# One core, all steps in a newly planned order: an attention block and a gated linear unit on TensorE

## The chip, the core and the metric

The kernel runs on one NeuronCore of one Trainium2 chip. A core has five engines that run their own instruction streams: TensorE (matmuls; PE in the profile, with its weight loads as PEld), VectorE (DVE), ScalarE (ACT), GpSimd (POOL) and SyncE (SP, here only a queue of DMA issues). They meet through semaphores. The metric is the device time of one execution in microseconds (us). The kernel before takes 303.13 us (median of three runs, 302.70 to 303.86).

## The reference

Inputs: q, k, v of shape (8 batches, 8 heads, 576 tokens, 64), a gain g_norm of 64, two 512x512 weights, and five rows of convolution weights of 512. The weights come in as 64-bit floats, and the kernel narrows them to 32 bits by integer arithmetic on the chip.

```python
kv  = einsum('bhsd,bhse->bhde', k, v)
out = einsum('bhsd,bhde->bhse', q, kv)
rms = sqrt(mean(out * out, axis=-1, keepdims=True) + 1e-06)
x   = (out / rms * g_norm)  # then (B, H, S, D) -> (B, S, H*D) = (8, 576, 512)

gate_pre[:, s] = sum over k of conv_w[k] * x[:, s - 4 + k]   # causal, zeros before s = 0
gate = 1.0 / (1.0 + exp(-gate_pre))
val  = x @ w_val
y    = (gate * val) @ w_out
```

## The kernel before, in words

Everything is in fp32. The work is cut into 1242 *steps*, each a small Python function that issues a few instructions. One string, PLAN, lists the steps in order, and a loop at the end of the kernel (`for step in PLAN.split(";")`) runs them as they stand there. No scheduler moves anything afterwards: each engine and each DMA queue executes its own instructions in the order of PLAN. The numbers behind an `@` say which buffers a step takes: PSUM banks (8 of them), tiles for normalised x (3), for output rows (`ot`, 4), for gates (4), and so on. If a buffer is still in use the step waits for its last reader.

The steps of one batch b, in the order of their data:

- **Loads.** `load_half k b i` and `load_half v b i` bring half the heads each. `load_q_rows` (batches 0 and 1) and `load_q` (the others, in four DMAs) bring q. `stage_weight` brings a quarter of a weight. Nearly all are issued on SP's queue, where the output stores are too.
- **k·v on quarters.** `kv_product b i` (line 475) has 36 small matmuls that use a 64x64 quarter of the array each; `kv_copy` (ACT) takes the result out. 
- **q·kv on quarters.** `turn_q` transposes q on DVE (in batch 1 `turn_q_rows` does it on PE, with half-width 128x64 matmuls, line 520). `raw_pair b c` (32 matmuls) and `raw_tail b` (8) are 64x64 as well (line 550). Batch 0 goes over `raw_half` (line 562).
- **Norm.** `square` (ACT), `sums` (DVE), `powers` (POOL, line 616), `normalise` (ACT, 16 small scalings to a `raw_pair`, line 635).
- **x transposed.** Batches 0 and 1 and all tails: `turn_x` on PE (line 647) and `keep_x` (ACT). Else `turn_blocks` (DVE) and `move_blocks` (8 DMAs to a batch's quarter set, on SP and POOL).
- **Gate.** `halo` (POOL), `gate_start` (ACT), four `gate_tap` (DVE, line 685), `gate_end` (ACT), `gated` (DVE).
- **Value product.** `val_product` (line 697) in batches 0 and 1; later `val_fast` in seven parts with `x_sums` on DVE ahead (a scheme with fewer multiplications) and `val_keep` behind, on ACT and DVE (line 746).
- **Output product.** To a pair of batches i: `token_sums` (DVE), then for each group p `fast_product i p 0..6` (line 837, full array) and `fast_keep i p 0..6` (ACT and DVE); `out_product i 8` (line 784, half-width) for the tail rows; `store`.

A `fast_product` of a group adds into the same bank as an earlier one: part 2 must come after `fast_keep` 0 has read the bank, part 4 after `fast_keep` 2, part 6 after `fast_keep` 4. Parts 1, 3 and 5 share another bank.

```python
        bank, tokens, weights_ = (        # fast_product, parts 0 to 6
            ("a", chunk(0, EVEN), wout[:, EVEN, LOW]), ("c", total(0), wsum[:, 0]),
            ("a", total(1), wsum[:, 1]), ("b", chunk(0, ODD), wout[:, ODD, LOW]),
            ("a", total(2), wsum[:, 2]), ("c", total(3), wout[:, ODD, HIGH]),
            ("a", chunk(1, ODD), wsum[:, 3]))[n]
```

(`b` and `c` are halves of one bank.) Three kinds of PE steps can be told apart by what they occupy: the **full array** (`turn_x`, `val_product`, `val_fast`, `fast_product`, most `raw_half`), **64x64 quarters** (`kv_product`, `raw_pair`, `raw_tail`), and **other part-width shapes** (`turn_q_rows` of batch 1, `out_product`, the tail of `raw_half`, `start_warm`, `turn_cw`). In this text an *excursion* is a stretch of PE's order in which it leaves full-array matmuls and comes back to them.

Of the kernel before, what the change touches and what calls it, by code (L numbers as in the profile page):

```python
# [31 lines left out]
narrow_weight wval 1 6 @ 1; load_half v 1 0; raw_half 0 4 0 @ 2; narrow_weight wval 0 3; sums 0 3 @ 0 0;
load_half k 1 1; raw_half 0 4 1; square 0 2 @ 1; narrow_weight wval 0 4; raw_half 0 0 0; powers 0 3;
narrow_weight wval 1 1; load_half v 1 1; raw_half 0 1 1; narrow_weight wval 0 7; square 0 4 @ 2;
square 0 0 @ 0; sums 0 2; narrow_weight wval 1 2; sums 0 4; load_half k 2 0 @ 0; normalise 0 3 @ 0;
narrow_weight wval 1 3; powers 0 2; sums 0 0; turn_q_rows 1 3 @ 0; square 0 1 @ 1; narrow_weight wval 1 4;
turn_x 0 3 @ 7; narrow_weight wval 3 0 @ 1; sums 0 1; turn_q_rows 1 0 @ 3; keep_x 0 3; load_half v 2 0 @ 0;
narrow_weight wval 3 1; normalise 0 2 @ 1; powers 0 1; turn_q_rows 1 1 @ 5; narrow_weight wval 1 7;
narrow_weight wval 3 2; load_half v 2 1 @ 0; turn_x 0 2 @ 7; normalise 0 4 @ 2; narrow_weight wval 3 3;
narrow_weight wval 2 5 @ 2; turn_x 0 4 @ 4; narrow_weight wval 2 0 @ 0; turn_q_rows 1 2 @ 2; keep_x 0 4;  # L40
narrow_weight wval 3 5 @ 0; keep_x 0 2; narrow_weight wval 3 6 @ 3; narrow_weight wval 2 1;
val_product 0 1 1 @ 4; narrow_weight wval 3 4; halo 0; narrow_weight wval 2 2; normalise 0 0 @ 0;
narrow_weight wval 2 3; normalise 0 1 @ 1; narrow_weight wval 3 7; sort_q 1 0 @ 1; turn_x 0 1 @ 7; sort_q 1 3;
narrow_weight wout 0 0 @ 1; turn_x 0 0 @ 6; narrow_weight wval 2 4; kv_product 1 0 @ 3 1; keep_x 0 0;
narrow_weight wout 0 5 @ 1; keep_x 0 1; narrow_weight wval 2 6 @ 0; gate_start 0 0 @ 0;
narrow_weight wout 0 6 @ 3; val_product 0 1 0 @ 0; narrow_weight wval 2 7; gate_start 0 2 @ 1;
narrow_weight wout 1 0 @ 0; gate_start 0 1 @ 2; gate_tap 0 0 3; narrow_weight wout 1 1; val_product 0 3 1 @ 6;
gate_tap 0 2 3; narrow_weight wout 0 1; gate_tap 0 1 3; narrow_weight wout 1 2; val_sums 2; gate_start 0 3 @ 3;
turn_q_rows 1 4 @ 7; gate_tap 0 2 2; sort_q 1 2; kv_product 1 1; load_q 2 1; gate_tap 0 3 3; gate_tap 0 1 2;
val_product 0 3 0 @ 2; kv_copy 1 1; kv_copy 1 0; sort_q 1 1; gate_tap 0 0 2; stage_weight wout 3 @ 0;  # L50
narrow_weight wout 0 2; load_q 2 2; gate_tap 0 1 1; narrow_weight wout 0 3; narrow_weight wout 1 5 @ 2;
raw_pair 1 3 @ 1 3; val_sums 0; sort_q 1 4; keep_val 0 1 0; narrow_weight wout 1 3; gate_tap 0 3 2; load_q 2 0;
raw_tail 1 @ 7 5; val_product 0 0 1 @ 0; keep_val 0 1 1; gate_tap 0 1 0; keep_val 0 3 1; square 1 4 @ 2;
gate_tap 0 3 1; square 1 3 @ 0; square 1 2 @ 1; sums 1 4 @ 1 1; raw_pair 1 1 @ 4 6; gate_tap 0 3 0;
keep_val 0 3 0; powers 1 4; gate_end 0 1; sums 1 2; val_product 0 2 0 @ 2; square 1 0 @ 2; sums 1 3;
keep_val 0 0 1; gated 0 1; normalise 1 4 @ 2; powers 1 3; val_sums 1; gate_end 0 3; turn_x 1 4 @ 0;
narrow_weight wout 3 5 @ 1; kv_product 2 0 @ 5 7; sums 1 0; keep_x 1 4; keep_val 0 2 0; powers 1 2;
square 1 1 @ 1; narrow_weight wout 1 4; val_product 0 2 1 @ 0; normalise 1 3 @ 1; narrow_weight wout 0 4;
sums 1 1; stage_weight wout 2 @ 1; narrow_weight wout 1 6 @ 0; load_half v 3 0 @ 0; powers 1 1;
normalise 1 2 @ 0; load_half k 3 0 @ 0; turn_x 1 3 @ 2; turn_q 2 1 @ 0; kv_product 2 1; gate_tap 0 0 1;  # L60
keep_x 1 3; powers 1 0; turn_x 1 2 @ 1; gate_tap 0 0 0; normalise 1 1 @ 2; val_product 0 0 0 @ 3;
narrow_weight wout 3 6 @ 2; turn_q 2 0; keep_x 1 2; halo 1; narrow_weight wout 0 7; normalise 1 0 @ 1;
load_q 2 3; turn_x 1 1 @ 2; narrow_weight wout 3 0 @ 1; val_product 1 3 1 @ 1; narrow_weight wout 1 7;
narrow_weight wout 2 0 @ 0; narrow_weight wout 3 1; gate_tap 0 2 1; load_half v 3 1 @ 0;
narrow_weight wout 2 1; load_half k 3 1 @ 0; narrow_weight wout 2 5 @ 1; val_product 1 0 1 @ 4; gate_tap 0 2 0;
keep_val 1 3 1; narrow_weight wout 3 2; val_sums 3; narrow_weight wout 3 3; gated 0 3; kv_copy 2 1;
val_product 1 2 1 @ 6; narrow_weight wout 2 2; turn_q 2 2; gate_end 0 2; turn_q 2 3; kv_copy 2 0;
keep_val 0 2 1; narrow_weight wout 3 4; gate_end 0 0; load_q 3 2; turn_x 1 0 @ 1; gated 0 2;
raw_pair 2 3 @ 7 5; keep_val 0 0 0; keep_val 1 2 1; gated 0 0; narrow_weight wout 2 3; raw_pair 2 1 @ 3 0;
square 2 3 @ 0; load_q 3 0; token_sums 0 0 0 @ 2; keep_val 1 0 1; val_product 1 1 1 @ 6; token_sums 0 0 1;  # L70
keep_x 1 0; keep_x 1 1; sums 2 3 @ 0 0; square 2 0 @ 2; load_q 3 1; narrow_weight wout 2 4; powers 2 3;
square 2 1 @ 1; weight_sums 0; val_product 1 2 0 @ 4; keep_val 1 1 1; sums 2 0; square 2 2 @ 0;
narrow_weight wout 3 7; gate_start 1 2 @ 2; powers 2 0; sums 2 1; kv_product 3 0 @ 2 1; keep_val 1 2 0;
sums 2 2; gate_start 1 0 @ 3; gate_tap 1 2 3; val_product 1 1 0 @ 6; normalise 2 3 @ 0; powers 2 2;
load_half k 4 0 @ 0; gate_tap 1 0 3; narrow_weight wout 2 6 @ 3; load_half v 4 0 @ 0; token_sums 0 0 2 @ 0;
powers 2 1; normalise 2 2 @ 2; fast_product 0 1 0 @ 4; narrow_weight wout 2 7; kv_product 3 1; weight_sums 1;
keep_val 1 1 0; turn_q 3 2 @ 1; raw_tail 2 @ 7 5; val_product 1 0 0 @ 6; weight_sums 2; square 2 4 @ 2;
kv_copy 3 0; turn_blocks 2 3; kv_copy 3 1; normalise 2 0 @ 1; turn_blocks 2 2; turn_q 3 0;
fast_product 0 1 1 @ 2; normalise 2 1 @ 0; turn_blocks 2 0; load_q 3 3; fast_product 0 1 3; gate_tap 1 0 2;
val_product 1 3 0 @ 1; fast_keep 0 1 0 @ 0; turn_q 3 1; gate_start 1 1 @ 1; turn_blocks 2 1; sums 2 4;  # L80
move_blocks 2 1; token_sums 0 0 3; fast_product 0 0 0 @ 0; keep_val 1 3 0; gate_tap 1 1 3; move_blocks 2 3;
fast_product 0 0 1 @ 3; fast_keep 0 0 0 @ 2; gate_tap 1 0 1; fast_keep 0 1 1 @ 1; gate_start 1 3 @ 0;
move_blocks 2 0; fast_product 0 0 3; gate_tap 1 0 0; keep_val 1 0 0; move_blocks 2 2; fast_product 0 1 5;
turn_q 3 3; gate_end 1 0; fast_product 0 1 2; weight_sums 3; fast_keep 0 0 1 @ 3; load_q 4 2; powers 2 4;
gate_tap 1 1 2; raw_pair 3 3 @ 1 6; fast_keep 0 1 2; gated 1 0; fast_product 0 0 2; square 3 2 @ 1;
gate_tap 1 1 1; square 3 3 @ 0; fast_keep 0 1 5; load_half v 4 1 @ 0; fast_product 0 1 4; normalise 2 4 @ 2;
sums 3 2 @ 1 1; fast_product 0 0 5; load_q 4 0; gate_tap 1 3 3; powers 3 2; turn_x 2 4 @ 2; fast_keep 0 1 4;
raw_pair 3 1 @ 7 5; keep_x 2 4; sums 3 3; fast_keep 0 0 2; x_sums 2 0 @ 0; fast_product 0 1 6; square 3 0 @ 2;
powers 3 3; store 0 2; gate_tap 1 3 2; square 3 1 @ 1; val_fast 2 1 0 @ 2; fast_keep 0 0 5; fast_keep 0 1 6;
# [824 lines left out]
```

## Time and profile before

| what | us |
|---|---|
| median of the runs | 303.13 |
| the profiled execution | 303.11 |
| its span, first to last instruction | 301.3 |
| PE busy | 290.3 |
| DVE busy | 272.0 |
| ACT busy | 194.5 |
| POOL busy | 114.1 |

Times in the views count from the start of the span. A PE row that is busy is not proof of useful work, since matmuls are pipelined and overlap: what counts is how far one start lies behind the one before. DMA moved 55.5 MB, at 359 GB/s in the first 30 us and at 184 on the mean.

### The profile page before, as it was taken

How to read it: one execution, taken by the hardware profiler on the slowest of the kernel's cores; microseconds unless marked ns; L12 is line 12 of the kernel's file. 1: busy time of each engine (PE TensorE's matmuls, PEld its weight loads, DVE VectorE, ACT ScalarE, POOL GpSimd, SP SyncE). 2: the span in 40 equal slices, each digit the busy share in tenths (PEclk: the TensorE clock that was granted, in tenths of full speed). 3: DMA queues.
4: the chain of work that ended last, by engine and by line, in shares of the span. 5: the costliest groups of instructions: out<-in, count | busy, mean ns of one | idle time of the engine just before them, and what ended most of it. 6: DMA issues, size and time to landing. Idle time of an engine off the chain costs nothing.

```text
span 301.3 us, 8755 instructions
## 1 busy us (share of the span) xinstructions
PE 290.3 (96%) x3333; PEld 227.9 (76%) x3333; DVE 272.0 (90%) x483; ACT 194.5 (65%) x606; POOL 114.1 (38%) x127
## 2 busy tenths in 40 slices
PE   6969999999999999999999999999999999999993
PEld 3658778778887768778778857788887588888572
DVE  2699999999999999999999899999999999999612
ACT  2887999998767957838864666557489244524320
POOL 3046029346578049218740296400693080000000
PEclk9998999999999999999999999999999999999999
DMA  7999686985678756966986669671650172311343
GB/s 266 373 385 413 245 244 203 297 228 184 154 191 222 243 146 143 315 180 165 268 208 221 184 140 303 173 208 30 165 115 17 34 168 70 82 43 29 94 114 105
DMA packets 32073, 55.51 MB, mean 184 GB/s; under 512 B 6166, under 2 KB 14358, under 8 KB 32032
## 3 DMA queue, kind: packets, MB, share of 16 engines
q1 hardware_dynamic: 29520, 49.76, 56.0%
q0 software_dynamic: 1632, 3.17, 4.9%
q10 hardware_dynamic: 880, 2.03, 1.8%
q8 instruction: 26, 0.43, 0.6%
q14 instruction: 15, 0.12, 0.1%
HBM read 39.21 MB, written 9.44 MB: 161 GB/s over the span
## 4 chain that ended last, share of the span: by engine, by line
PE 82%; DMA 12%; SPq 3%; ACT 1%; issue 0%; DVE 0%; ACTq 0%
PE bank L837 28%; PE bank L746 24%; PE bank L697 11%; DMA qs<-in_q_dram 7%; PE bank L550 6%; PE bank L475 5%; PE bank L784 5%; DMA out_dram<-ot 3%; DMA v<-in_v_dram 2%; PE bank L647 2%; PE bank L520 2%; SPq L869 1%; SPq L381 1%; SPq L366 1%; ACT ot L851 0%
## 5 line engine op out<-in xcount | busy, mean ns | idle before, releaser
L685 DVE SCALAR_TENSOR_TENSOR gate<-xT,cwT,gate 128x576 f32<-128x576 f32 x128 | 101.3, 807 | 0.9
L616 POOL TENSOR_TENSOR rt<-ss,mhalf 128x8 f32<-128x8 f32 (+3 forms) x38 | 70.1, 1854 | 59.6 <-DVE ss L606 59.5
L635 ACT ACTIVATE x<-bank,rt 128x64 f32<-128x64 f32 x252 | 55.8, 365 | 6.8 <-POOL rt L616 6.7
L668 POOL DMA_DIRECT2D xT<-y x48 | 26.6, 559 | 72.5 <-PE bank L837 38.4
L837 PE MATMUL bank<-wsum,w 128*128 128x256 f32 x192 | 47.0, 383 | 0.9 <-ACT ot L853 0.8
L837 PEld LDWEIGHTS bank<-wsum,w 128*128 128x128 f32 x192 | 35.6, 190 | 7.9 <-ACT ot L853 1.9
L746 PE MATMUL bank<-xs,vsum 128*128 128x288 f32 x144 | 38.5, 407 | 0.0
L697 PE MATMUL bank<-xT,wval 128*128 128x288 f32 x128 | 33.9, 413 | 0.0
L837 PE MATMUL bank<-wout,gv 128*128 128x256 f32 x128 | 32.6, 380 | 0.3 <-ACT ot L851 0.3
L746 PEld LDWEIGHTS bank<-xs,vsum 128*128 128x128 f32 x144 | 27.1, 190 | 7.3 <-DVE gv L753 0.2
L599 ACT ACTIVATE sq<-bank 128x256 f32<-128x256 f32 (+1 forms) x70 | 21.0, 374 | 12.9 <-PE bank L550 12.8
L697 PEld LDWEIGHTS bank<-xT,wval 128*128 128x128 f32 x128 | 23.4, 190 | 6.3 <-ACT xT L654 0.2
L837 PEld LDWEIGHTS bank<-wout,gv 128*128 128x128 f32 x128 | 24.2, 190 | 4.3 <-ACT ot L851 0.4
L606 DVE TENSOR_REDUCE ss<-sq 128x8 f32<-128x520 f32 (+1 forms) x40 | 24.8, 627 | 2.2 <-ACT sq L599 2.2
L746 PE MATMUL bank<-xT,wval 128*128 128x288 f32 x96 | 26.4, 408 | 0.0
L847 DVE TENSOR_TENSOR ot<-bank,ot 128x512 f32<-128x512 f32 (+1 forms) x32 | 17.1, 548 | 10.1 <-DMA out_dram<-ot 9.2
L679 ACT ACTIVATE gate<-xT,cwT 128x576 f32<-128x576 f32 x32 | 25.7, 809 | 0.5 <-DVE gv L710 0.2
L692 ACT ACTIVATE gate<-gate 128x576 f32<-128x576 f32 x32 | 22.1, 704 | 5.0 <-DVE gate L685 5.0
L710 DVE TENSOR_TENSOR gv<-gv,gate 128x576 f32<-128x576 f32 x32 | 23.5, 750 | 1.0 <-ACT gate L692 0.7
L746 PEld LDWEIGHTS bank<-xT,wval 128*128 128x128 f32 x96 | 18.0, 190 | 4.5 <-ACT x L635 0.2
L550 PEld LDWEIGHTS bank<-kv,qT 64*64 64x64 f32 x1008 | 16.3, 135 | 5.7 <-issue 3.7
L475 PEld LDWEIGHTS bank<-v,k 64*64 64x64 f32 x1008 | 16.0, 135 | 4.0 <-issue 1.6
(93 smaller groups left out, 454.0 us busy)
## 6 DMA issues: line engine op xcount, KB each, us to landing
qs<-in_q_dram SPq DMA_DIRECT2D x96, 140.0 KB, 3.8
out_dram<-ot SPq DMA_DIRECT2D x140, 64.0 KB, 1.8
k<-in_k_dram SPq DMA_DIRECT2D x14, 576.0 KB, 5.4
v<-in_v_dram SPq DMA_DIRECT2D x12, 576.0 KB, 6.3
xT<-y SPq DMA_DIRECT2D x48, 64.0 KB, 2.6
xT<-y POOLq DMA_DIRECT2D x48, 64.0 KB, 2.4
y<-in_moe_w_val_dram SPq DMA_DIRECT2D x4, 512.0 KB, 11.6
w<-in_moe_w_out_dram SPq DMA_DIRECT2D x4, 512.0 KB, 7.4
```

Of the source, the lines that this page charges most:

```text
L475: nc.tensor.matmul(st["kvps", b][s][r * D:(r + 1) * D, i], st["k", b, i][rows, r, cols], st["v", b, i][rows, r, cols], start=(j == 0), sto ...
L550: nc.tensor.matmul(st["raw", b, c][r][cols, to * D:(to + 1) * D], st["qT", b][rows, hp, first:first + D], kvs[b % 2][rows, hp, :], start=T ...
L606: nc.vector.reduce_sum(out=st["ss", b][:, FIRST[c]:FIRST[c] + n], in_=st["sq", b, c][:, 0:n], axis=AX.X)
L616: nc.gpsimd.tensor_tensor(out=st["rt", b][:, which], in0=st["ss", b][:, which], in1=mhalf[:, which], op=ALU.pow)
L635: nc.scalar.activation(out=x[:, to * D:(to + 1) * D], in_=raw[:, h * D:(h + 1) * D], func=AF.Copy, scale=root[:, to:to + 1])
L668: (nc.sync if i % 2 else nc.gpsimd).dma_start(out=xTs[b % 2][i * TB:(i + 1) * TB, :, first:first + P], in_=y[a * TB:(a + 1) * TB, i])
L679: nc.scalar.activation(out=gate[:], in_=xTs[b % 2][:, jt, HALO:SX], func=AF.Copy, scale=cwT[:, K - 1, jt:jt + 1])
L685: nc.vector.scalar_tensor_tensor(out=gate[:], in0=xTs[b % 2][:, jt, tap * TB:tap * TB + S], scalar=cwT[:, tap, jt:jt + 1], in1=gate[:], op ...
L697: nc.tensor.matmul(val[:], wval[:, kc, jt * P:(jt + 1) * P], xTs[b % 2][:, kc, HALO + n * SV:HALO + (n + 1) * SV], start=(kc == 0), stop=( ...
L710: nc.vector.tensor_tensor(out=both, in0=both, in1=st["gate", b, jt][:], op=ALU.mult)
L746: nc.tensor.matmul(st[bank, "val", b, mj][:], weights_[:, k], tokens()[:, k], start=(n in (0, 1, 3) and k == 0), stop=(k == NK // 2 - 1), ...
L837: nc.tensor.matmul(st[bank, i, p], tokens()[:, k], weights_[:, k], start=(n < 2 and k == 0), stop=(k == NK // 2 - 1), skip_group_check=True)
```

## The change

The functions stay as they are. PLAN is replaced as a whole: it has the same 1242 steps with the same arguments in another order, with other buffers behind the `@`. The first eleven steps and the last eight are as before.

What the new order does, read out of both:

- **Excursions.** PE's order before has 30: 22 that begin with a 64x64 step, 7 with a half-width step and 1 with `start_warm`. The new order has 24: 16, 6, 1, and 1 with `turn_cw`. The halves of `kv_product` of batches 0 to 4 now follow each other, before each half stood alone, or beside a `raw_tail` or a `turn_q_rows`; in batch 7 the two halves and `raw_tail 6` follow each other; both `raw_pair` and the tail of batch 1 form one stretch, and three of the four first `turn_q_rows 1`. The pair of `raw_pair 4` comes apart.
- **Opening.** `turn_q_rows 0` comes in the order of chunks 3, 4, 0, 2, 1 (before 2, 4, 1, 0, 3), `load_q_rows 1` stands ahead of `stage_weight wval 3`, `stage_weight wval 2` right behind it, and `load_half k 1` behind the weights wout 0 and 1 and `load_half v 1`. `kv_product 0 1` comes ahead of all `raw_half`.
- **From there on** the steps of all engines and queues are interleaved anew.

The diff, cut to its core:

```diff
-stage_weight cw 0 @ 0; stage_weight wval 3; turn_q_rows 0 2 @ 1; turn_q_rows 0 4 @ 2; sort_q 0 2 @ 0;
-turn_q_rows 0 1 @ 3; sort_q 0 4; turn_q_rows 0 0 @ 4; turn_q_rows 0 3 @ 5; sort_q 0 1; start_warm 3 256 @ 6;
-sort_q 0 3; load_q_rows 1 1; load_q_rows 1 0; narrow_weight cw 0 5 @ 0; sort_q 0 0; kv_product 0 0 @ 0 7;
-narrow_weight cw 0 6 @ 1; narrow_weight cw 0 0 @ 0; start_warm 1 256 @ 2; kv_half 0 0; narrow_weight cw 0 1;
-raw_half 0 1 0 @ 1; narrow_weight cw 0 2; kv_product 0 1; narrow_weight cw 0 3; narrow_weight cw 0 4;
...
-narrow_weight wout 3 5 @ 1; kv_product 2 0 @ 5 7; sums 1 0; keep_x 1 4; keep_val 0 2 0; powers 1 2;
...
-normalise 1 2 @ 0; load_half k 3 0 @ 0; turn_x 1 3 @ 2; turn_q 2 1 @ 0; kv_product 2 1; gate_tap 0 0 1;
...
-fast_keep 1 3 1 @ 1; sums 7 0; fast_keep 1 2 2; fast_product 1 2 3; fast_keep 1 3 2; token_sums 1 1 3;
-square 7 1 @ 2; move_blocks 6 0; gate_tap 5 0 2; fast_product 1 2 4; sums 7 1; fast_product 1 3 4;
...
-fast_keep 3 2 5; fast_product 3 3 2; store 3 4; fast_keep 3 2 6; fast_product 3 3 3; fast_keep 3 3 1 @ 0;
-fast_keep 3 3 2; fast_product 3 3 4; store 3 5; fast_product 3 3 5; fast_keep 3 3 4; fast_product 3 3 6;
...
+stage_weight cw 0 @ 0; turn_q_rows 0 3 @ 1; turn_q_rows 0 4 @ 2; turn_q_rows 0 0 @ 3; sort_q 0 4 @ 0;
+turn_q_rows 0 2 @ 4; turn_q_rows 0 1 @ 5; sort_q 0 0; start_warm 3 256 @ 6; load_q_rows 1 0; load_q_rows 1 1;
+narrow_weight cw 0 5 @ 0; sort_q 0 2; stage_weight wval 3; kv_product 0 0 @ 0 7; sort_q 0 3;
+stage_weight wval 2; narrow_weight cw 0 0 @ 0; sort_q 0 1; narrow_weight cw 0 1; narrow_weight cw 0 2;
+kv_product 0 1; narrow_weight cw 0 3; kv_half 0 0; start_warm 1 256 @ 2; narrow_weight wval 0 0 @ 1;
...
+kv_product 2 1 @ 6 0; normalise 1 3 @ 1; narrow_weight wout 0 7; powers 1 2; narrow_weight wout 3 6 @ 3;
+kv_product 2 0; val_sums 3; keep_val 0 0 1; square 1 1 @ 0; narrow_weight wout 1 4; val_product 0 2 1 @ 5;
...
+fast_product 1 3 4; store 2 3; sums 7 1; powers 7 3; gate_tap 5 0 1; fast_product 1 3 3; fast_keep 1 3 1 @ 1;
+fast_keep 1 2 2; fast_keep 1 3 4; fast_product 1 2 4; gate_tap 5 2 1; powers 7 1; normalise 7 3 @ 2;
...
+fast_keep 3 3 0 @ 2; fast_product 3 2 4; fast_keep 3 2 5; fast_product 3 3 2; store 3 4; fast_keep 3 2 4;
+fast_product 3 2 6; fast_keep 3 3 2; fast_product 3 3 4; fast_keep 3 3 1 @ 0; fast_keep 3 2 6;
```

More of the change, by code (lines that the diff above doesn't have):

```diff
@@ L32 @@
[L32 to L52, printed above, removed]
@@ L63 @@
[L63 to L82, printed above, removed]
@@ L83 @@
[L83 to L87, printed above, removed]
@@ new lines @@
+gate_tap 1 2 2; square 2 0 @ 1; kv_product 3 0; narrow_weight wout 2 6 @ 0; powers 2 3; keep_val 1 2 0;
+normalise 2 2 @ 1; narrow_weight wout 2 4; val_product 1 3 0 @ 1; token_sums 0 0 3 @ 1; load_half v 4 0 @ 0;
+token_sums 0 0 2; narrow_weight wout 3 3; powers 2 1; sums 2 0; kv_copy 3 1; kv_copy 3 0; normalise 2 3 @ 0;
+gate_tap 1 1 3; fast_product 0 0 1 @ 4; turn_q 3 0 @ 1; powers 2 0; val_product 1 0 0 @ 0;
+narrow_weight wout 3 4; normalise 2 1 @ 2; load_q 3 3; turn_blocks 2 3; narrow_weight wout 3 7;
```

336 lines of the change are left out of this document (189 added, 147 removed).

## The prediction, made blind

> **What bounds the kernel now.** First the page: TensorE (PE) is busy 96% of the span, VectorE (DVE) 90%, and both fill nearly all slices between the opening and the end. The chain that ended last runs over PE for 82%.
>
> ```profile
> PE 290.3 (96%) x3333; PEld 227.9 (76%) x3333; DVE 272.0 (90%) x483; ACT 194.5 (65%) x606; POOL 114.1 (38%) x127
> ...
> PE   6969999999999999999999999999999999999993
> ...
> DVE  2699999999999999999999899999999999999612
> ...
> PE 82%; DMA 12%; SPq 3%; ACT 1%; issue 0%; DVE 0%; ACTq 0%
> ```
>
> Then the waits of PE. There are few: one on the q rows of batch 1 in the opening, one near the end.
>
> ```profile
> PE bank L520 <- DMA qs<-in_q_dram: 2.3, 1, 2.3
> ...
> PE bank L837 <- ACT ot L853: 0.8, 1, 0.8
> ...
> PE bank L837 <- ACT ot L851: 0.3, 1, 0.3
> ```
>
> So between 31 and 293 us the end is set by PE's own work. What of that is lost shows in the chain in order of time (start, length, what):
>
> ```profile
> 43.61 1.09 PE bank L550 x64
> ...
> 52.64 1.94 PE bank L697 x8
> ...
> 61.28 2.02 PE bank L550 x128
> 63.30 4.08 PE bank L697 x16
> 67.38 1.21 PE bank L475 x72
> ```
>
> Quarter records: 64 take 1.09 us, 128 take 2.02, so 64 more cost 0.93 (14.6 ns each) and a stretch has 0.16 on top, however long; 72 fit (1.05 + 0.16 = 1.21). Full ones: 8 undisturbed take 1.94, so 16 would take 3.88; between two excursions they take 4.08, 0.20 more. **An excursion costs 0.16 + 0.20 = 0.36 us** beside its records.
>
> The second engine is nearly as full. In the stretches from 30 to 270 us DVE is busy 234.9 of 240 us (two of the eight shown; columns: us, PE, PEld, DVE):
>
> ```profile
> 120.00:150.00 30.00, 30.00 (x395) 23.98 (x394) 29.32 (x52) 21.57 (x76) 15.42 (x21) 1.00 0.84 232
> 150.00:180.00 30.00, 29.73 (x398) 22.72 (x398) 28.92 (x50) 17.88 (x58) 11.60 (x13) 1.00 0.71 188
> ```
>
> It idles 5.1 us there, mostly for what PE, or ACT behind it, has not delivered (2.2 us for squares). That is all the room it has.
>
> **The change, part by part.** No instruction is added or removed, so only places and waits count.
>
> *Excursions.* 30 become 24: 6 x 0.36 = **-2.14 us** (0.356 unrounded). Two fall away in the opening, four behind it.
>
> *Does DVE keep up?* I put each PE and DVE instruction at the sum of the rows ahead of it on its own engine (start to start: 0.243 us per record of L746 and L697, 0.216 of L837, 0.0146 in quarters, 0.36 per excursion; DVE a row's duration less 0.08 overlap, 0.115 more behind its own operand). In the profile before, PE runs 7.1 us behind its sum from 31 to 280 us, within 0.6. DVE runs 10.7 behind at first and 15.3 behind at the end, and 4.8 of that are 16 waits, so the sums are true. The difference of both offsets (3.6 at first, 7.3 at 190, 8.2 at the end) must not exceed the *lead*: PE's sum at the step that reads less DVE's sum at the step that writes. The smallest lead per 12 us before: 5.1 at 81, 6.0 at 136, 7.5 at 202, with 3.6 to 7.3 needed. In the new order: 3.8 at 83, 3.7 at 90, 4.0 at 118, 4.2 at 140 to 209, 4.6 at 220, 5.9 at 248. PE has come nearer to DVE by one to three us. The reverse condition, DVE waiting for PE, has eased alike: where before it forced the difference up to 5.9 at 129 and 7.4 at 192, it now asks for 4.0 and 4.6. So DVE need not idle before 200 us, but it may not idle either: between both conditions lie some 0.2 to 0.8 us.
>
> *Opening.* The q rows of batch 1 go ahead of wval 3 on SP's queue: 512 KB less in front, at 1.3 to 1.4 us for that much in the landings (wval 0 at 13.78, 1.28 behind v 0 1), so 19.4 instead of 20.81. PE, with all ten raw_half now behind kv_product 0 1 (its end at 13.97, then 0.6 warm-up, 40 records of L562 at 0.116, switches and turn_cw 0.6), is done with them at 19.8, not 18.5. So of the 2.3 us wait 1.05 is won. Then PE waits for VectorE's normalised chunks: val_product 0 1 1 comes at about 26.9, 6.75 behind its sum, not 7.1. On DVE the sorting copies come 2 us later, in time that was idle; the weights start at the landing of wval 0 (13.78) with 3.05 in front, an offset of 10.8, and up to 0.4 more if wval 1 still lands at 16.44. I take 10.95, 0.25 later than before. k 1 0 stands behind four others more (two halves of v, two weights: 2.2 MB), by bytes at 30.4 instead of 25.05, needed at 34.8: covered. POOL's powers come in another order and end at 21.8, 23.9 and 26.8, each before its reader.
>
> *Together.* At PE's sum 90 the lead of 3.7 (3.87 with the 0.2 by which direct leads came out short in the profile before) asks for a PE offset of 10.95 - 3.87 = 7.1: the opening's 0.35 is given back, net **0.0** (from -0.35 with no DVE delay to +0.4 with all of it).
>
> *The stall near the end.* fast_product 3 3 4 waits for fast_keep 3 3 2, which stands on ACT behind fast_keep 3 3 1, which waits for the end of fast_product 3 3 3. PE's timeline (start, length):
>
> ```profile
> 291.18 1.03 PE L837 MATMUL bank<-wsum,w 128*128 128x256 f32 x4
> 292.04 1.03 PE L837 MATMUL bank<-wout,gv 128*128 128x256 f32 x4
> 293.85 1.13 PE L837 MATMUL bank<-wsum,w 128*128 128x256 f32 x4 [0.78 <-ACT ot L853]
> ```
>
> and ACT's timeline at the same place:
>
> ```profile
> 293.15 0.37 ACT L851 COPY ot<-bank 128x256 f32<-128x256 f32 x1 [1.34 <-PE bank L837]
> 293.42 0.38 ACT L853 COPY ot<-bank 128x256 f32<-128x256 f32 x1
> ```
>
> 1.81 from start to start where 0.86 is usual: 0.95 lost. In the new order fast_product 3 2 6 stands between and fast_keep 3 3 2 goes first: **-0.95**. But the same pattern now stands at PE's sum 209 (fast_product 1 3 3, fast_keep 1 3 1, 1 2 2, fast_product 1 2 4): **+0.95**. SP's stores stay in time in both places (landing 1.7 us after the issue).
>
> *Rest.* With so little room between both conditions, DVE and ACT rows that vary by 0.03 to 0.1 us will cost PE some small waits. The trace before has some 0.4 us of such (0.3 at 217, the others below 0.1 each). Bounds for the increase: 0 and 0.8, the room itself; I take **+0.3**, nearer to the row.
>
> Sum: -2.14 + 0 - 0.95 + 0.95 + 0.3 = -1.84 on the profiled execution's 303.11 (the median of the runs is 303.13): **301.3 us**.
>
> **The rivals.**
> *VectorE becomes the bound (slower).* If DVE keeps until PE's sum 197 the idle time that it had before, the difference is 7.3 + 0.25 against a lead of 4.4 there: PE is 3.1 late, 303.11 - 2.14 + 3.1 = 304.1. It decides from 2.1 us on, more than half of that idle time. For it: leads of about 4 over 120 us. Against it: its idle time came from waits for PE that the order no longer asks for.
> *The opening makes DVE late.* If wval 1 is slowed by the q rows behind it and lands with them near 18, DVE starts 1.5 later, and the leads hand all of it to PE: 302.8. For it: transfers that overlap in flight (wval 1 took 2.66 us behind wval 0).
> *The stall at 209 does not come*, since ACT or the store is early or PE is late there anyway: 300.4. Against it: the same four steps in the same order.
> *The excursions do not cost by themselves*, but by operands that come late: no gain, 301.3 + 2.1 = 303.4. Against it: the fixed part is the same in every stretch.
> *PSUM empties too slowly.* ACT has 4 squares and 16 scalings per raw_pair, 4 x 0.30 + 16 x 0.22 = 4.7 us against 0.93 on PE; where two pairs newly follow each other (batch 1) the second's 4.7 us, less the one val_product of 1.94 that PE has next, would be waited for: 301.3 + 2.8 = 304.1. Against it: the 128 records at 61.28 are such a neighbourhood, and PE goes on at 63.30 without a wait. The Trainium skill, TensorEngine Tiling (Array Packing), section Performance Considerations, says that tiling speeds up TensorE but not the emptying of PSUM, which may become the bottleneck; by that rule this rival would win, and the trace does not bear it out here.
>
> **How the numbers follow.** Chances: forecast 0.50, DVE 0.10, opening 0.14, no stall 0.17, no excursion cost 0.05, PSUM 0.04. 0.5% (1.5 us) is about what a measurement can tell from no change, so faster means under 301.6. The forecast's own range is 300.7 to 302.2 and two thirds of it lie under 301.6 (0.34); with the missing stall (0.17) and a little of the opening case: faster 0.53. Slower, over 304.65, needs DVE or PSUM at more than the price above: 0.06. Same: 0.41. The range takes in the missing stall and the opening, and half of the DVE case: 300.2 to 303.4.
>
> **What would show it.** Right: 24 excursions at 0.36 each, quarter stretches of 144 records at 2.26 us; PE's busy time shorter by about 2; DVE idle between 30 and 200 us down from some 4 to about 1; a PE wait of 0.8 on L853 near 216 us and none near the end; the first L697 at about 26.9. Wrong: many short PE waits on DVE or ACT lines between 90 and 220 us (DVE is the bound), or DVE's weight rows starting later than 14.

## The result and the profile after

The changed kernel takes 304.15 us (median of 21 runs, 303.73 to 305.89) where the kernel before, on the same chip, takes 302.58 (21 runs): a ratio of 1.0047, interval 1.0031 to 1.0063. It is half a per cent slower; the forecast was 0.6% faster. The profiled execution took 304.69 us, its span 302.9; like the one before (303.11) it lies 0.5 us above its kernel's median, so the difference of the two spans, 1.6 us, is that of the medians.

The first two parts of the page after (busy time, PE in slices) and the chain that ended last:

```profile
PE 288.6 (95%) x3333; PEld 226.4 (75%) x3333; DVE 271.9 (90%) x483; ACT 193.5 (64%) x606; POOL 115.5 (38%) x127
...
PE   6897998999999999999999999999999999999992
...
PE 62%; DVE 13%; DMA 8%; ACT 7%; SPq 5%; issue 2%; POOL 1%; DVEq 0%; ACTq 0%
```

PE is busy 1.7 us less, as the forecast wanted, and yet the span is 1.6 longer. The chain tells why: PE carries 62% of it instead of 82%. DVE, ACT and POOL are in it now, which they hardly were. The waits of PE (line waited at, who released it; us in total, times, longest) name the places (the two longest, in the first 13 us, are left out):

```profile
...
PE bank L648 <- DVE x L626: 1.3, 1, 1.3
PE bank L515 <- DMA qs<-in_q_dram: 1.2, 1, 1.2
PE bank L698 <- ACT gv L707: 0.8, 1, 0.8
PE bank L838 <- ACT ot L854: 0.7, 1, 0.7
PE bank L648 <- ACT wexp L409: 0.7, 1, 0.7
PE bank L698 <- ACT sq L600: 0.6, 1, 0.6
...
```

To see what each place is worth, I take again PE's *offset*: the start of an instruction less the sum of the rows ahead of it on PE. It grows by what PE loses. (Line numbers after are one higher than before.)

| where, by the profiled executions | us |
|---|---|
| PE's own sum, 289.00 before and 286.87 after | -2.14 |
| opening, offset 7.1 before and 7.08 after at 31 us | 0.0 |
| 49.03: val_product 0 2 1 waits for its bank, behind ACT | +0.98 |
| 65.49: no data is late (below) | +0.73 |
| 70 and 90: small steps | +0.4 |
| 219.17: the forecast stall, fast_product 1 2 4 | +0.90 |
| 225.9, 275.6, 278.6: waits for ACT and DVE | +0.9 |
| the stall of fast_product 3 3 4 near the end is gone | -0.95 |
| behind the end of PE's last matmul: 4.62 before, 5.48 after | +0.86 |
| sum; the spans give 302.9 - 301.3 = 1.6 | +1.7 |

The steps add up to the difference of the spans within 0.1 us. Some of the forecast's rows stand there as drawn. The chain has the doubled stretches (start, length, what), 144 quarter records in 2.26 us:

```profile
102.19 2.26 PE bank L476 x144
```

and PE's timeline has the stall that was forecast at the sum 209, where fast_product 1 2 4 waits for fast_keep 1 2 2:

```profile
217.41 1.03 PE L838 MATMUL bank<-wout,gv 128*128 128x256 f32 x4
219.17 1.13 PE L838 MATMUL bank<-wsum,w 128*128 128x256 f32 x4 [0.74 <-ACT ot L854]
```

DVE is fuller than before in the middle, as the leads asked for (by stretch: us, PE, PEld, DVE, ACT, POOL, then PE's granted clock, DMA's share and GB/s), with 0.1 to 0.4 us idle in 30 where it was 0.7 and 1.1:

```profile
120.00:150.00 30.00, 30.00 (x396) 24.03 (x395) 29.62 (x53) 21.33 (x78) 16.40 (x18) 1.00 0.79 222
150.00:180.00 30.00, 30.00 (x399) 22.95 (x398) 29.93 (x53) 18.31 (x57) 14.77 (x17) 1.00 0.71 196
```

**The wait at 49 us** comes from POOL. The chain in order of time:

```profile
41.42 2.73 POOL rt L617
44.14 0.02 issue
44.16 0.93 ACT x L636 x4
45.09 0.29 ACT gv L707
45.38 1.10 ACT sq L600 x4
46.48 0.57 ACT gate L693
47.06 1.63 ACT x L636 x8
48.69 0.30 ACT gv L707
48.99 0.04 issue
49.03 0.99 PE bank L698 x3
```

The power of the four tail columns (powers 1 4) takes 2.73 us; powers of four columns elsewhere in the two traces take 1.0 to 1.7. Beside it DVE runs two rows of the weights (L412, L422, 0.69 each). ACT waits 1.73 us for it, then does everything in a row, and the copy that frees PE's bank (keep_val 0 0 1) stands behind the eight scalings of normalise 1 3. PE cannot take another bank: raw_tail 1 and both raw_pair of batch 1, now one stretch, took six of the eight.

**The gap at 65.49** is put down to a square, but the bank's last reader, the copy keep_val 1 2 1, ended at 61.04. PE's timeline:

```profile
60.68 2.09 PE L551 MATMUL bank<-kv,qT 64*64 64x64 f32 x128
62.71 2.21 PE L698 MATMUL bank<-xT,wval 128*128 128x288 f32 x8
65.49 2.21 PE L698 MATMUL bank<-xT,wval 128*128 128x288 f32 x8 [0.57 <-ACT sq L600]
```

A queue of the page that the prediction never looked at is nearest to it:

```profile
q8 instruction: 26, 0.43, 0.6%
```

That is 26 transfers of about 16.5 KB, one for every 256 instructions of PE (3333 weight loads, 3333 matmuls and 93 others make 26.4 times 256). One runs from 62.65 to 63.96, and PE goes on 1.5 us later, at an instruction where, by count, a new block begins (the count is under a_fetch). By the rows above, quarter records use up a block fast (two instructions in 14.6 ns: 256 in 1.9 us; full-array work needs some 30 us), and the stretch ahead of 62.7 is 128 of them.

**The last stores.** DVE's last copy ends at 297.90 (before 297.17). One of SP's last stores then waits for another store:

```profile
SPq L870 <- DMA out_dram<-ot: 1.5, 1, 1.5
```

In the traces the stores of both queues take eight completion semaphores in turn, and a store goes only when the one before with its semaphore has landed. SP's third last store waits for one that ACT's queue issued at 297.39 and that landed at 299.17; it goes at 299.19, the last at 300.02, landing at 301.76. Before, the last went at 298.54 and landed at 300.17.

### The profile page after: what moved, and what is told of

The parts are those of the page before. It is cut to its first block, busy times and chain, and to the rows that moved or that the text cites. A ratio compares the mean times of both kernels' runs of the same rounds, so it can differ in the third digit from the quotient of the medians.

```text
span 302.9 us, 8741 instructions
## 1 busy us (share of the span) xinstructions
PE 288.6 (95%) x3333; PEld 226.4 (75%) x3333; DVE 271.9 (90%) x483; ACT 193.5 (64%) x606; POOL 115.5 (38%) x127
## 4 chain that ended last, share of the span: by engine, by line
PE 62%; DVE 13%; DMA 8%; ACT 7%; SPq 5%; issue 2%; POOL 1%; DVEq 0%; ACTq 0%
PE bank L838 25%; PE bank L747 19%; DMA k<-in_k_dram 6%; PE bank L698 5%; DVE gate L686 5%; PE bank L785 5%; PE bank L476 4%; PE bank L551 4%; SPq L358 2%; SPq L669 2%; ACT x L636 2%; DMA v<-in_v_dram 1%; DMA qs<-in_q_dram 1%; ACT sq L600 1%; POOL rt L617 1%
## 5 line engine op out<-in xcount | busy, mean ns | idle before, releaser
L617 POOL TENSOR_TENSOR rt<-ss,mhalf 128x8 f32<-128x8 f32 (+3 forms) x38 | 70.9, 1877 | 62.6 <-DVE ss L607 62.1
L747 PE MATMUL bank<-xs,vsum 128*128 128x288 f32 x144 | 39.3, 409 | 0.2 <-ACT gv L756 0.2
L848 DVE TENSOR_TENSOR ot<-bank,ot 128x256 f32<-128x256 f32 (+1 forms) x32 | 17.3, 549 | 10.5 <-ACT ot L850 6.1
L747 PE MATMUL bank<-xT,wval 128*128 128x288 f32 x96 | 26.3, 407 | 0.2 <-DMA v<-in_v_dram 0.2
L607 DVE TENSOR_REDUCE ss<-sq 128x8 f32<-128x520 f32 (+1 forms) x40 | 24.5, 631 | 1.0 <-ACT sq L600 0.9
L476 PEld LDWEIGHTS bank<-v,k 64*64 64x64 f32 x1008 | 15.9, 135 | 4.7 <-issue 1.7
```

The source lines that it names most:

```text
L476: nc.tensor.matmul(st["kvps", b][s][r * D:(r + 1) * D, i], st["k", b, i][rows, r, cols], st["v", b, i][rows, r, cols], start=(j == 0), sto ...
L607: nc.vector.reduce_sum(out=st["ss", b][:, FIRST[c]:FIRST[c] + n], in_=st["sq", b, c][:, 0:n], axis=AX.X)
L617: nc.gpsimd.tensor_tensor(out=st["rt", b][:, which], in0=st["ss", b][:, which], in1=mhalf[:, which], op=ALU.pow)
L747: nc.tensor.matmul(st[bank, "val", b, mj][:], weights_[:, k], tokens()[:, k], start=(n in (0, 1, 3) and k == 0), stop=(k == NK // 2 - 1), ...
```

## The experiments

Two theories for the loss. *Places*: each wait in the table costs what it shows, and mending it pays that. *Ring*: PE, ACT, POOL and DVE hold each other up, since none has room; a mended wait comes back elsewhere until the end, and only what lies at the end pays in full. All ratios are to the kernel before, run on the same chip.

**a_keep: the bank's copy ahead of the scalings.**

```diff
 kv_product 2 1 @ 6 0
+keep_val 0 0 1
 normalise 1 3 @ 1
 ...
-keep_val 0 0 1
 square 1 1 @ 0
```

> The changed plan with keep_val 0 0 1 moved ahead of normalise 1 3 on ScalarE, nothing else. In the profile of the changed kernel PE waits until 49.03 us for bank 5 (0.98 us late against its own sum of rows), because this copy stands behind eight scalings of 0.2 us. Theory of the places (each stall of PE is lost by itself): that wait disappears and the time falls by about 0.8 us, to 303.3. Rival (VectorE bounds the new order, so PE is only made to wait for it at about 90 us instead): the wait at 49 goes, one of 0.5 to 0.9 us appears between 60 and 95 us on a VectorE or xT tile, and the time stays at 304.1.

304.46 us against 302.88: 1.0048 [1.0029, 1.0066]. PE's wait for L707 is gone from the table, and nothing is gained. In this trace PE's clock fell in the opening (a digit 7 in its fourth slice): PE is 1.64 us behind a_tail's trace (below) at 28 us, and 0.85 from 49 us to its last matmul, so its trace does not show what the other engines would take back. The median says that mending the place alone brings nothing.

**a_fetch: PE's instructions counted otherwise.** The warm-up ahead of all work has 34 short matmuls in place of 5 long ones; this moves every later instruction by 116 places in its block of 256.

```diff
-start_warm 5 256 @ 0
+start_warm 34 32 @ 0
```

> The changed plan with start_warm 5 256 replaced by start_warm 34 32: 29 warm-up products more, each narrower, in the idle time before the q rows land; they add 116 instructions to PE's stream and nothing to its work behind 6.3 us. In the profile of the changed kernel PE stands still from 64.75 to 65.49 us although the semaphore it waits on has its value since 61.04; a 16 KB block of PE's instructions starts to arrive 1.8 us after the place where such blocks are asked for, in the middle of a stretch of quarters. Theory (PE waits for its own instructions): the blocks' borders move by 116 instructions, the border no longer falls 270 instructions behind the start of that stretch, the stall of 0.73 disappears, 303.4. Rival (it waits for bank 1 or for ScalarE after all, as the table of waits says): the stall of 0.6 to 0.75 stays at the same step and the time stays at 304.1.

309.92 us, 1.0222 [1.0194, 1.0249]. The gap at 65 is gone, and new ones stand where the border now falls into quarter records. PE's timeline of a_fetch:

```profile
12.46 1.14 PE L476 MATMUL bank<-v,k 64*64 64x64 f32 x58 [1.60 <-DMA v<-in_v_dram]
15.83 0.68 PE L476 MATMUL bank<-v,k 64*64 64x64 f32 x14 [2.23 <-issue]
...
193.30 0.91 PE L476 MATMUL bank<-v,k 64*64 64x64 f32 x43 [0.74 <-issue]
```

"Issue" means that the profile shows nothing that PE waited for. Instruction transfers ran from 13.29 to 14.43 and from 190.83 to 191.88: PE goes on 1.40 and 1.42 us after their ends. Over all traces there are nine such gaps (0.2 to 2.5 us), all in kernels of the new order, all at the same place in the count of 256 (the 193rd or 194th, counted over PE's weight loads, matmuls and semaphore instructions in the trace), 1.3 to 1.6 us behind a transfer's end; the old order's kernels have none. So late instructions cost time, and the borders' places decide where. How much of a_fetch's 7 us they are can be read from its trace, by the start of the same PE instruction in a_tail (below): a_fetch is 2.4 us later behind the first gap, 3.9 when a_tail is at 18 us (a_fetch's granted clock is 0.50 from 15.9 to 19.3 us of its own time), 3.1 while a_tail goes from 24 to 178 us, and 5.1 at the last matmul. The second gap is 0.95 of that, a wait for ACT at 218 us another 0.8. So the two gaps are 3.4 of the 5.1 us.

The Trainium skill, Runtime: NRT & Kernel Launch, section Instruction fetch mechanics, says that PE's instructions come in blocks of 16 KiB (256 instructions), fetched while the one before runs, and that the cost of a border is mostly hidden. The size agrees with the 26 transfers. "Mostly hidden" holds for the 3333 matmuls of the old order, not for all of the new one's long stretches of quarter records.

**a_tail: the new order with its last two full stores split over both queues.**

```diff
-store 3 4
+store_last 3 4 1; store_last 3 4 0
 ...
-store 3 5
+store_last 3 5 1; store_last 3 5 0
```

> The changed plan with the stores of blocks 3 4 and 3 5 shared between SP's and ScalarE's queues (two each) as those of 3 6 and 3 7 are already. Nothing before 285 us changes. In the profile of the changed kernel SP's last three stores are issued at 299.19, 299.60 and 300.02, the first of them 1.55 us late: the stores carry eight semaphores in turn, and this one's had last been given to a store on ScalarE's queue that landed at 299.17. Theory (the end is set by that wait): no store waits for one that was issued in the last 2 us, the last one lands about 1.3 us earlier, 302.8. Rival (the last stores wait for VectorE's last addition, which ends at 297.90, and for nothing else that matters): 304.1, no change.

303.68 us, 1.0018 [0.9995, 1.0042]; 0.7 to 0.9 us less than the changed kernel in executions of the same mean clock (0.998 or 1.0: spans of 301.2 to 301.4 against 301.9 to 302.1). Behind the end of PE's last matmul stand 4.56 us, not 5.48. The last stores go at 297.98 and 298.05. This trace has PE's wait at 49 but no gap at 65 (its block's transfer ended at 61.25 instead of 63.96), so that gap is not in every execution. PE's timeline at the same place:

```profile
60.81 2.09 PE L551 MATMUL bank<-kv,qT 64*64 64x64 f32 x128
62.84 4.15 PE L698 MATMUL bank<-xT,wval 128*128 128x288 f32 x16
```

**b_fk: the old order without its stall near the end.**

```diff
 fast_product 3 3 3
+fast_keep 3 3 2
 fast_keep 3 3 1 @ 0
-fast_keep 3 3 2
 fast_product 3 3 4
```

> The plan before, with fast_keep 3 3 2 ahead of fast_keep 3 3 1 and nothing else: it takes away the stall of 0.95 us near the end (fast_product 3 3 4) that the prediction counted as won. Theory of the prediction's sum: the stall goes and the time falls by 0.95 us, to 301.6. Theory that the end is set by the stores' semaphores: PE ends 0.9 us earlier, but the stores on ScalarE's queue now take their semaphores three places earlier in the turn, SP's third last store waits for one of them to land, and the time stays at 302.5 to 302.7.

302.42 us, 0.9979 [0.9959, 0.9999]. PE's stall is gone from the trace, but of 0.95 us only 0.46 arrive in the time. The rest goes into the same wait of stores as in the changed kernel. SP's waits in b_fk, in a line that has 0.6 in the kernel before:

```profile
SPq L869 <- DMA out_dram<-ot: 1.5, 1, 1.5
```

**b_end: both repairs of the end on the old order.** The swap of b_fk and the split of a_tail together.

```diff
-store 3 4
+store_last 3 4 1; store_last 3 4 0
 fast_keep 3 2 6
 fast_product 3 3 3
+fast_keep 3 3 2
 fast_keep 3 3 1 @ 0
-fast_keep 3 3 2
 fast_product 3 3 4
-store 3 5
+store_last 3 5 1; store_last 3 5 0
```

> The plan before with fast_keep 3 3 2 ahead of fast_keep 3 3 1 (which alone brought 0.46 us of the 0.95 it takes off PE) and the stores of blocks 3 4 and 3 5 shared between SP's and ScalarE's queues. Theory (the rest was eaten by a store that waits for a semaphore of a late store on the other queue): no store waits for one issued in the last 2 us, the last lands 0.8 to 1.3 us earlier than in the plan before, 301.6 to 302.0, and with it the kernel beats both plans. Rival (the stores' waits cost nothing by themselves): as with the swap alone, 302.4.

**301.45 us against 302.86: 0.9963 [0.9940, 0.9986]**, faster than either plan. Here 1.4 us arrive for a stall of 0.95 and a wait of stores: at the end of the kernel nothing stands behind that could take it back.

b_end also shows what the forecast's base had in it. In windows of the opening the kernel before (columns: us, PE, PEld, DVE, ACT, POOL, then PE's granted clock, DMA's share and GB/s)

```profile
14.00:22.00 8.00, 5.49 (x53) 4.90 (x53) 7.43 (x18) 7.14 (x15) 3.09 (x2) 0.96 1.06 380
22.00:30.00 8.00, 8.00 (x72) 6.44 (x69) 7.93 (x17) 5.75 (x10) 5.22 (x6) 0.82 1.04 412
```

and b_end, with the same steps there:

```profile
14.00:22.00 8.00, 5.46 (x54) 4.78 (x55) 7.37 (x17) 7.13 (x15) 3.06 (x2) 1.00 1.06 381
22.00:30.00 8.00, 7.75 (x78) 5.89 (x80) 7.93 (x17) 6.53 (x11) 5.81 (x6) 1.00 1.04 413
```

The profiled execution before had a mean clock of 0.82 in these 8 us; in finer windows it is 0.50 from 21.5 to 24.5 us and 1.00 from 25 on. In b_end PE comes out of the opening 6.2 behind its sum, not 7.1, and has drifted to 6.74 at 73 us. The new order starts at 7.08 at full clock: its opening is 0.9 us worse at 31 us, 0.3 to 0.4 at 80.

**a_dvek and b_dve: is it DVE?** From each order two gate taps (0.73 us of DVE each) of batch 0 are left out, so two terms of the convolution are missing. a_dvek also has a_keep's move.

```diff
-gate_tap 0 1 1
 ...
-gate_tap 0 0 2
```

> The changed plan with keep_val 0 0 1 ahead of normalise 1 3 (which alone brought nothing) and two of VectorE's gate taps of batch 0 left out (gate_tap 0 1 1 and 0 0 2, about 40 us): 1.46 us less work on VectorE, nothing less on TensorE; the output lacks these two terms. Theory (VectorE's lead bounds PE up to 90 us: PE may not come nearer to VectorE's offset than some 3.5 us, wherever it has been held up before): VectorE's offset behind 45 us falls by up to 1.46, PE waits less before 95 us, and the time falls by 1.0 to 1.4 us, to about 303. Rival (PE's stalls at single places, by banks and ScalarE, set the end and VectorE has room): the time stays at 304.1 to 304.5.

> The plan before with the same two gate taps left out (gate_tap 0 1 1 and 0 0 2), so the output lacks these terms: 1.46 us less on VectorE before 45 us. If VectorE's lead binds PE only in the new order, as the prediction had it (smallest leads 5.1 before, 3.7 after), the time stays at 302.6 to 302.9. If it binds in the old order too (in one profile of the old plan PE came out of the opening 1 us earlier and was at the same offset of 7.0 by 73 us), the time falls by 0.4 to 0.9 us.

a_dvek 303.87 us against 302.86, 1.0028 [1.0007, 1.0048]; b_dve 302.67, 0.9991 [0.9971, 1.0011]. Of 1.46 us taken from DVE the new order returns 0.3 to 0.6 (against the changed kernel and a_keep), the old one about 0.2, by medians whose intervals overlap. The traces say more. At 90 us PE's offset is 7.86 against a_tail's 8.65, and 0.62 of these 0.79 are left at PE's last matmul. In the old order, against b_end's trace, the two taps move PE by 0.5 us between 43 and 62 us, and 0.3 of it are left from 177 us on. So DVE's work holds PE in both orders, not in the new one alone. DVE itself now waits in a_dvek (0.63 us at 42.6 for squares, 0.52 at 58.4 for q rows). DVE is one link, not the bound.

**a_cwk and a_cw2: the opening's rows on DVE.** Before, three small rows (keep_cw, 0.6 us) filled DVE's wait for the weight wval 1; in the new order they come at 19.6, since PE's turn_cw stands behind kv_half and raw_half. a_cwk puts turn_cw and keep_cw right behind the weight that they need, a_cw2 also moves one raw_half behind them; both have a_keep's move.

```diff
-raw_half 0 0 1 @ 4        # a_cw2 only
 ...
 narrow_weight cw 0 7
+turn_cw @ 5
+keep_cw
+raw_half 0 0 1 @ 4        # a_cw2 only
 ...
-turn_cw @ 5
 ...
-keep_cw
```

> The changed plan with keep_val 0 0 1 ahead of normalise 1 3 and with turn_cw and keep_cw right behind narrow_weight cw 0 7, so that VectorE has its three small rows of keep_cw (0.6 us) to do where the new order leaves it idle for 0.76 us until wval 1 has landed (15.9 to 16.7 us). Theory (VectorE's late opening, by way of its lead): VectorE's offset behind the opening falls from 11.3 to about 10.75, as before the change, PE's at 90 us by as much, and the time by 0.5 to 0.65 us, to 303.6. Rival (the opening's delay has no part in it): 304.1 to 304.4, and VectorE idles for as much elsewhere before 30 us.

> The changed plan with keep_val 0 0 1 ahead of normalise 1 3 and turn_cw, keep_cw one raw_half earlier than in the first attempt (ahead of raw_half 0 0 1), so that PE turns cw at about 16.0 us and VectorE copies it while it waits for wval 1. Theory (the opening's delay of VectorE reaches the end): VectorE's offset behind 18 us is 10.8 to 10.9 instead of 11.3, PE waits 0.4 us less at 24 to 26 us, and the time falls by 0.3 to 0.5 against 304.13 to 304.46. Rival: it is waited for again before 90 us, 304.1 to 304.5.

a_cwk 304.13 against 302.86, 1.0040 [1.0025, 1.0055]: DVE now waits 0.8 us for PE's turn_cw, so the edit did not do what it should. a_cw2 303.95 against 302.25, 1.0055 [1.0037, 1.0073]: DVE waits 0.33 and its offset falls to 11.07, PE's wait at 24 us is 0.8 instead of 1.3, and two gaps for instructions appear (0.2 and 0.4). No gain in the time.

**a_powk and a_pow2: POOL's power without the rows beside it.** DVE's order is changed so that gate taps stand beside powers 1 4; both runs also have a_keep's move. In a_powk a piece of wout is narrowed from another quarter's data, behind a load that DVE then waits for; its time (305.83 against 302.67, 1.0104 [1.0057, 1.0150]) says nothing on the question.

> The changed plan with keep_val 0 0 1 ahead of normalise 1 3, and on VectorE two gate taps and sums 1 3 ahead of narrow_weight wout 0 4 and wout 1 6. In the profile of the changed kernel POOL's powers 1 4 took 2.71 us with these two narrowing rows beside it; the same four columns took 1.01 to 1.20 in seven of twelve places, with gate taps beside them. ScalarE stood idle for 1.73 us before normalise 1 4 for it. Theory (POOL's power beside VectorE's two-tensor rows makes ScalarE late, and by it PE at 49 us): powers 1 4 takes 1.1 to 1.5 us, ScalarE's idle time shrinks to under 0.5, PE does not wait between 42 and 52 us, and the time falls by 0.6 to 1.0 from that of the plan with the copy alone moved (304.46), to 303.6. Rival (PE is held by VectorE's sum of work by 90 us in any case): ScalarE comes earlier but the time stays at 304.1 to 304.4.

a_pow2 puts that right (a_keep's move is not shown again):

```diff
 square 1 3 @ 0
+normalise 1 4 @ 2; gate_tap 0 1 0; sums 1 3; gate_tap 0 3 1
 narrow_weight wout 0 4
 narrow_weight wout 1 6 @ 2
-normalise 1 4 @ 2
+load_q 2 2
 stage_weight wout 2 @ 1
-sums 1 3; load_q 2 2; gate_tap 0 1 0
 ...
-gate_tap 0 3 1
```

> As the run before it with VectorE's rows reordered beside powers 1 4, but with stage_weight wout 2 and load_q 2 2 in the order that lets narrow_weight wout 0 4 read what it should and not wait for a load. Theory (POOL's power beside two-tensor rows makes ScalarE late, and by it PE): powers 1 4 takes 1.0 to 1.5 us instead of 2.71, ScalarE waits under 0.6 us before normalise 1 4 instead of 1.73, PE waits under 0.3 us in sum between 42 and 55 us instead of 0.8 to 1.1, the time falls by 0.6 to 1.0 against the plan with only the copy moved (304.46), to 303.6. Rival (all four engines are tied in a ring, and what is won here is waited for by 90 us): PE's offset at 90 us is within 0.3 of that without the change, 304.1 to 304.5.

304.65 against 302.25, 1.0066 [1.0046, 1.0086]. POOL's timeline and PE's in a_pow2:

```profile
41.56 1.52 POOL L617 TENSOR_TENSOR rt<-ss,mhalf 128x4 f32<-128x4 f32 x1 [12.40 <-DVE ss L607]
```

```profile
46.45 1.40 PE L476 MATMUL bank<-v,k 64*64 64x64 f32 x80
48.82 0.87 PE L476 MATMUL bank<-v,k 64*64 64x64 f32 x45 [0.97 <-issue]
```

The first two links are right: with other rows of DVE beside it the power takes 1.52 instead of 2.73, and ACT's wait falls from 1.73 to 0.20. The third, from ACT to PE at 49 us, rests on the chain shown above: PE's wait there is gone in a_pow2, but a_keep's move alone takes it away too, and no run has the power mended without that move. PE now reaches the quarter records of kv_product 2 earlier than their instructions and loses 1.2 there, and at 90 us its offset is 9.4, no better than the changed kernel's 9.3.

The Trainium skill, SBUF — State Buffer, section Who interferes with whom, says that a DVE instruction with two SBUF inputs contends with a GpSimd instruction that reads SBUF, over a pair of ports that one of the two holds alone. The two rows of the weights add 1.2 us of their 1.4, which agrees. The gate taps have two such inputs as well, and beside two of them (1.54 us) the power took 1.52, at most 0.5 over the shortest ones: there it agrees badly, and the measurement stands.

**a_best, a_best2 and b_best: all repairs at once.** a_best narrows the same piece of wout from another quarter's data as a_powk. a_best2 is the new order with a_cw2, a_pow2, a_tail and the swap at 219:

```diff
 fast_product 1 3 3
+fast_keep 1 2 2
 fast_keep 1 3 1 @ 1
-fast_keep 1 2 2
```

b_best is b_end with two gate taps of batch 0 earlier, so that they stand beside POOL's powers:

```diff
 keep_val 0 0 1
+gate_tap 0 0 1; gate_tap 0 0 0
 gated 0 1
```

> All repairs of the changed plan together: the reordering of VectorE's rows beside powers 1 4 and keep_val 0 0 1 earlier, fast_keep 1 2 2 ahead of fast_keep 1 3 1 (the stall of 0.90 us at 219 us), and the stores of 3 4 and 3 5 shared between two queues (which alone brought 0.5 to 0.9). If the stalls of single places set the end, they add up: 0.7 + 0.5 (0.9 less what VectorE takes back) + 0.7, time 302.2 or less. If VectorE's and ScalarE's late rows take back what PE wins, the stores' share alone remains: 303.5.

> All repairs of the changed plan at once, this time without the slip in the order of stage_weight wout 2: turn_cw and keep_cw earlier, VectorE's rows beside powers 1 4, keep_val 0 0 1 earlier, fast_keep 1 2 2 ahead of fast_keep 1 3 1, stores of 3 4 and 3 5 on two queues. If the places add up, 0.4 + 0.7 + 0.5 + 0.7 less than 304.3: 302.0, no slower than the plan before and 0.5 above the repaired old plan (301.45). If the ring of engines takes it back, 303.3 to 303.6, the stores' share alone.

> The plan before with both repairs of its end (301.45) and gate_tap 0 0 1 and 0 0 0 moved ahead of gated 0 1 on VectorE, so that no two-tensor row lies beside powers 1 3, which took 3.02 us there against 1.63 alone; POOL runs four powers in one row there (43.2 to 53.5 us), and PE waits 0.2 to 0.3 us each for scalings on ScalarE at 50 and 72 us. Theory (POOL's powers bound ScalarE, and by it PE, there): powers 1 3 takes 1.7 to 2.2, POOL's row ends 0.8 us or more earlier, and the time falls by 0.3 to 0.7, to 301.0. Rival (the powers that follow are stretched instead, the rows only change places): 301.4 to 301.7.

a_best 304.23 against 302.67 (1.0056 [1.0026, 1.0086]); a_best2 302.78 against 302.25 (1.0012 [0.9995, 1.0029]); b_best 302.82 against 302.67 (1.0004 [0.9974, 1.0034]), 1.6 us behind b_end's distance to the kernel before. In a_best2 the next powers of POOL are stretched instead, and PE waits for their scalings:

```profile
43.18 6.69 POOL L617 TENSOR_TENSOR rt<-ss,mhalf 128x8 f32<-128x8 f32 x2 [0.55 <-DVE ss L607]
```

```profile
50.89 1.58 PE L648 MATMUL bank<-ident,x 128*128 128x128 f32 x8 [1.00 <-ACT x L636]
```

In b_best POOL's powers are shorter (2.14 us, not 3.02), but the taps stand ahead of turn_q, q's next loads come later, and DVE waits 3.4 us for them, PE behind it:

```profile
63.59 1.40 PE L550 MATMUL bank<-kv,qT 64*64 64x64 f32 x80 [1.08 <-DVE qT L499]
```

How much of a mended place is kept can be read from the traces: all kernels of the new order have the same 3333 matmuls, so the start of the same matmul can be compared. The table has it less its start in a_tail, whose order before 290 us is the changed kernel's and whose trace has the wait at 49 (0.99) and no gap at 65. All runs but the changed kernel have a_keep's move.

| us later than in a_tail at | 47 | 49 | 62 | 90 | 219 | last |
|---|---|---|---|---|---|---|
| changed kernel | 0.00 | -0.13 | -0.13 | +0.68 | +0.66 | +0.65 |
| a_cwk | +0.09 | -0.90 | +0.06 | +0.04 | +0.18 | +0.17 |
| a_cw2 | +0.39 | -0.60 | -0.44 | -0.41 | -0.26 | -0.25 |
| a_pow2 | +1.69 | +0.75 | +0.75 | +0.74 | +0.75 | +0.75 |
| a_dvek | +0.20 | -0.79 | -0.79 | -0.79 | -0.61 | -0.62 |
| a_best2 | -0.49 | -1.48 | +0.23 | +0.23 | -0.27 | -0.02 |

Neither theory holds alone. The move wins 0.94 to 0.99 us at 49 each time. In a_cwk and a_best2 all of it is lost again by 52 us, where `turn_x` (L648) waits for the scalings that now stand behind the copy: ACT comes late to them there, by its wait of 1.83 us for POOL in a_cwk and by waits of 1.04 and 0.70 us for the row of 6.69 in a_best2. In a_cw2, a_dvek and a_pow2, where ACT waits 1.18, under 0.2 and 0.20 us for that power, most or all of the move's gain is kept up to 90 us; but a_pow2 has lost 1.6 us to its two gaps for instructions (0.4 at 41.5 us, 1.2 at 48.8) and a_cw2 0.6 to its own. So in these traces a mended wait came back where the next link was late, and not elsewhere. The gap at 65 stays lost to the end. Behind 90 us the swap at 219 wins 0.71 us, and 0.46 of it is left at the last matmul. With all repairs a_best2 ends about where a_tail alone does (1.0012 and 1.0018), and b_end is faster than both against the kernel before.

## Why the prediction was wrong, step by step

- **Excursions, -2.14: right.** PE's busy time fell by 1.7, stretches of 144 took 2.26 as drawn. The price of 0.36 holds in the new order: PE passes six excursions between 110 and 170 us, and with that price its offset is the same at both ends to 0.1 us.
- **Does DVE keep up, 0: right in size, too narrow in question.** DVE idles less in the middle (2.1 us from 30 to 200 where it was 3.4; about 1 was forecast), and no PE wait of weight there names DVE. But I asked only whether DVE is late for PE. At 49 us it was DVE's rows that slowed POOL, POOL that made ACT late, and ACT that kept PE's bank.
- **Opening, 0.0: wrong by its base.** PE's offset came out as said (7.08 to 7.1), the first L697 at 27.4 (26.9 said), DVE's offset at 11.3 to the 10.95 taken. But the 7.1 of before held a clock at half speed for some 3 us, seen in a digit 8 of the clock's row that I passed over; at full clock the old opening gives 6.2, and 6.7 by 73 us. So 0.3 to 0.9 us that the old order has at full clock were not in my base. Of the kernel before's 108 executions beside the experiments, the 33 with a mean clock of 0.999 or 1.0 have a median of 302.15, the 44 with 0.994 or less one of 302.87.
- **The stall moved, -0.95 and +0.95: right.** 0.90 measured at the new place, none at the old.
- **"SP's stores stay in time in both places": wrong, +0.86, counted as nothing.** I knew 1.7 us from issue to landing, but not that a store waits for another queue's store with the same semaphore. a_tail gives 0.9 back, and b_fk shows the same trap in the old order: only with the stores split does the stall's end arrive.
- **Rest, +0.3 with bounds 0 and 0.8: the term that failed, +3.0 measured** (0.98, 0.73, 0.4 and 0.9). Its upper bound was the room between PE's and DVE's conditions, which caps only waits of those two for each other. The wait at 49 runs over POOL, ACT and a bank; the one at 65 is for instructions. The row that I went by was misread too: in the trace before such waits, from start to start, are 0.34 at 163.5 us (the L851 that I put at 217), 0.21 at 186.4 and 0.26 at 217.7, 0.8 in all and not 0.4.
- **The rivals.** Two of them, VectorE as the bound and PSUM, were priced at 304.1, next to the 304.15 measured; that is chance, since neither's sum is what was lost. VectorE as the bound did not come: its idle time shrank. The opening's DVE delay came in small (0.35 more than taken), as a wait for wval 1 of 0.8 in a_tail; in the changed kernel's own trace wval 1 came earlier and ACT's row was waited for, 0.48. PSUM emptied too slowly at a neighbouring place: where I looked (61 us) PE went on; at 49 PE waited for a bank that ACT had not read. By the rule of the Trainium skill, TensorEngine Tiling (Array Packing), section Performance Considerations, that tiling speeds up TensorE and not the emptying of PSUM, this was to be feared; the trace agrees with 0.98 us at that place, though ACT was late there by its wait of 1.73 for POOL, and the 2.8 that I priced did not come.

What stays open: how often the gap at 65 comes (it is in one of the two traces with that code unchanged up to there and a full clock), and whether the power mended alone would take away PE's wait at 49.

## What to carry to other kernels

An order that packs short instructions closer saves TensorE's own time, but the kernel gains it only if the engines behind it have room: where several engines are nearly full, look for what each *removed gap* had been covering, and expect that a mended wait may return as another a few microseconds on. What stood behind the last matmul paid in full here, so begin there: split the last stores over two queues, and see that none waits for another's landing. Before subtracting from a profile, read its clock row: one digit of 8 was a microsecond here.

## What the runs showed that was not expected

- Late instruction blocks: gaps of 0.2 to 2.5 us with no late data, always at a border of 256 PE instructions, 1.3 to 1.6 us behind the end of a 16.5 KB transfer. Eight of the nine stand in stretches of quarter records, the one at 65.49 eight full-array matmuls behind such a stretch.
- A clock at half speed for 3.4 us in the opening of some executions (21.4 to 24.8 us in the profile before, 26.3 to 29.7 in a_keep, 15.9 to 19.3 in a_fetch), which a row in tenths over slices of 7.5 us shows as one digit of 8 or 7.
- POOL's power row of 4 columns took 1.0 to 1.7 us in other places and 2.73 beside two rows of the weights; two rows of 8 columns took 6.69 together in a_best2, 4.26 in b_best.
- Stores of two queues share eight completion semaphores: a store with nothing else to wait for stood 1.55 us until another queue's store had landed.
